# A fused attention and feed-forward kernel on one core: softmax 576 wide, values in 128-token chunks, another planner

## Chip, cores, metric

The kernel runs on one core of one Trainium2 chip. The metric is device time in microseconds (us), lower is better. Times are medians of several runs. In the profiles PE is TensorE (matmul), PEld its weight loads, DVE is VectorE, ACT is ScalarE, POOL is GpSimd and SP is the engine that issues most DMAs.

## The reference, cut to what matters

```python
# q, k, v: (8 batches, 8 heads, 576 tokens, 64); p: (8, 8, 32, 64); float32
def sm_attn(qq, kk, vv):
    s = scale * matmul(qq, kk.T)                  # scale = 1/8
    a = exp(s - max(s)); a = a / (sum(a) + 1e-9)
    return matmul(a, vv)
p_packed = sm_attn(p, k, v)                       # first softmax, over 576 tokens
x = sm_attn(q, p_packed, p_packed)                # second softmax, over 32 packed tokens
h = maximum(x @ w_in, 0)                          # x as (4608, 512), w_in (512, 2048)
out = (h * h) @ w_out                             # (2048, 512)
```

The kernel never forms `x`. Per batch it computes M = p_packed @ w_in once ("M chunks"), and the second softmax's weights times M give the hidden layer ("feed-forward groups" F1, 16 per batch). The squared result times w_out gives the output ("output matmuls" F2, 576 in all).

## The kernel before

A small planner inside the kernel takes steps with costs, dependencies and buffer slots, and decides in which order each engine gets its instructions. On the chip the order is then fixed.

```python
# sums of the first softmax, and what follows them (VectorE, in this order)
def extract(self):                       # packed values, PSUM -> SBUF, needed by M
    ...                                  # 4 copies of 64x64
def recip(self):
    nc.vector.reciprocal(self.rD, ps[:, 256:258])            # 128x2, from PSUM
    nc.vector.tensor_scalar_mul(self.rD8, self.rD, 0.125)    # 128x2, SBUF -> SBUF
def pq_block(self):                      # "block copies": operand of the second softmax
    ...                                  # 8 copies of 32x64, PSUM -> SBUF
# second softmax, per half (288 of 576 queries), PSUM tiles of one bank (pool "a")
S2:  ps_a <- pq, qT      exp(scale=rD8) on ScalarE -> e2
N:   ps_a <- ones_bd, e2  Ln, then Exp(scale=-1) on ScalarE; VectorE multiplies e2 by it
# feed-forward, PSUM tiles of two banks (pool "h", two tiles)
F1:  ps_h <- M, a2        relu on ScalarE (0.65 us) -> r;  gT = r*r on VectorE
F2:  ps_o <- gT, w_out    16 matmuls per 128 tokens
# casts of k, q, v to bf16 on GpSimd; v in 96-token chunks (6 groups)
```

The softmax here doesn't subtract the row's maximum and nothing guards it: scores larger than these inputs give would overflow.

## Time and profile before

The median was 286.82 us of 3 runs (285.31 to 287.47). The profiled execution itself took 288.86 us, so its absolute sums are a little high.

| | before |
|---|---|
| span of the profiled run | 287.1 us |
| TensorE busy | 248.8 us (87%) |
| VectorE / ScalarE / GpSimd busy | 183.8 / 173.6 / 78.3 us |
| TensorE matmuls | 1920 |

First the page of the kernel before: busy time by engine, and the TensorE and clock rows of the picture in 40 slices (tenths of each 7.2 us slice).

```profile
PE 248.8 (87%) x1920; PEld 141.1 (49%) x1920; DVE 183.8 (64%) x360; ACT 173.6 (60%) x333; POOL 78.3 (27%) x120
PE   0527958689969979997999799999999999999993
PEclk9999986979979999999999999999999999999999
```

The next table cuts the same run into stretches. Columns: start and end, length, busy time (and instructions) of TensorE, its weight loads, VectorE, ScalarE and GpSimd, then the granted clock, the DMA share and GB/s.

```profile
0.00:20.00 20.00, 4.55 (x60) 4.45 (x60) 12.45 (x33) 8.35 (x13) 7.13 (x23) 1.00 0.96 306
20.00:40.00 20.00, 15.52 (x136) 8.67 (x137) 15.44 (x25) 15.51 (x31) 8.72 (x7) 1.00 1.05 346
40.00:60.00 20.00, 14.54 (x86) 6.93 (x86) 17.72 (x31) 11.31 (x24) 11.00 (x11) 0.77 1.07 319
60.00:100.00 40.00, 37.27 (x309) 22.49 (x307) 32.79 (x53) 24.59 (x48) 24.99 (x47) 0.94 0.88 255
100.00:280.00 180.00, 174.53 (x1322) 97.72 (x1321) 105.38 (x221) 113.28 (x218) 26.42 (x35) 1.00 0.33 94
```

Length minus TensorE busy is the hole: 15.5, 4.5, 5.5, 2.7 and 5.5 us. From 60 us on TensorE is nearly full, so every hole there lengthens the run, and so does every matmul.

Who makes the holes after 40 us? These are TensorE's waits in that stretch (waiting line, what released it: total us, times, longest).

```profile
PE ps_a L365 <- DVE pq_bd_101 L339: 4.4, 3, 2.4
PE ps_o L422 <- POOL w_out_b L175: 3.5, 3, 2.5
PE ps_a L365 <- DVE pq_bd_102 L339: 3.5, 2, 1.8
PE ps_o L422 <- DVE gT L414: 2.3, 2, 1.3
```

The two lines with `pq_bd` are the second softmax (L365) waiting for VectorE's block copies: 7.9 us together. One such wait, in order of time, shows what delays the copies (start, duration, engine, line, instruction):

```profile
74.75 2.87 POOL L175 CAST v_b<-v_f 96x1536 bf16<-96x1536 f32 x2
74.97 0.17 DVE L329 RECIPROCAL rD<-ps_pp 128x2 f32<-128x2 f32 x1
75.17 3.57 DVE L330 TENSOR_SCALAR rD_1058<-rD 128x2 f32<-128x2 f32 x1
77.58 2.23 POOL L175 CAST q_b<-kq_f 128x1152 bf16<-128x1152 f32 x2
78.65 1.36 DVE L279 STREAM_TRANSPOSE kT<-k_b 128x1152 bf16<-128x1152 bf16 x1
79.95 1.83 DVE L339 CAST pq_bd_101<-ps_pp 32x64 bf16<-32x64 f32 x8
81.58 0.69 PE L365 MATMUL ps_a<-qT,pq_bd_101 128*128 128x288 bf16 x2 [2.42 <-DVE pq_bd_101 L339]
```

The multiply of 128x2 numbers is recorded at 3.57 us, the reciprocal of the same size just before it at 0.17. The multiply ends at 78.74; GpSimd's first q cast began at 77.58 and a q cast takes 1.14 us, so it ended at 78.72. The multiply sat through the rest of three GpSimd casts. This repeats in five of the eight batches (3.57, 3.17, 2.95, 3.13 and 1.91 us). In the first batch the multiply takes 0.96 us beside one cast, and in the other two 0.17, with no cast or one that was just ending. The cause of the meeting is in the program: the end of the value matmuls frees the v buffer for GpSimd's casts and gives VectorE its sums at the same moment.

The hole that ends at 81.58 us has a second cost. Here are two stretches, just before and just after its end (columns as in the table above), and two groups of matmuls 288 wide, the first within the second stretch and the other after it:

```profile
78.20:81.60 3.40, 0.98 (x6) 0.26 (x4) 3.29 (x10) 0.07 (x1) 3.40 (x4) 1.00 1.00 257
81.60:85.00 3.40, 3.40 (x15) 2.09 (x16) 2.24 (x6) 1.69 (x4) 0.40 (x1) 0.51 1.03 262
82.54 2.13 PE L399 MATMUL ps_h<-a_662,M 128*128 128x288 bf16 x8
85.56 0.65 PE L399 MATMUL ps_h<-a_662,M 128*128 128x288 bf16 x4
```

After the hole the granted clock was 0.51 for 3.4 us. TensorE was busy all that time, but its matmuls started 240 ns apart; the later four started 122 to 123 ns apart. So a busy TensorE can lose time too: a stretch whose clock is under 1.00 holds less work than its busy time says.

### The profile page before, as it was taken

Reading aid. Unit: us, or ns where it says so; the run is one execution under the profiler, and the core shown is the slowest. Engines: PE = TensorE matmul, PEld = TensorE weight load, DVE = VectorE, ACT = ScalarE, POOL = GpSimd, SP = SyncE. Lnnn points to the kernel's source line nnn. Section 1 sums busy time; section 2 is a strip of 40 time slices with the busy share of each in tenths; the row PEclk is TensorE's granted clock in tenths of the full one; section 3 lists DMA queues with packets and bytes.
Section 4 is the critical chain, followed back from the end, with each engine's and each line's share of the span. In section 5 each row is a group of like instructions: output and inputs, shape, how many; then the busy total and the mean of one; then the engine's idle time right before and its main releaser. Section 6 shows DMA issues by size and latency. Waiting matters only on the chain.

```text
span 287.1 us, 5281 instructions
## 1 busy us (share of the span) xinstructions
PE 248.8 (87%) x1920; PEld 141.1 (49%) x1920; DVE 183.8 (64%) x360; ACT 173.6 (60%) x333; POOL 78.3 (27%) x120
## 2 busy tenths in 40 slices
PE   0527958689969979997999799999999999999993
PEld 0512624346535634573547354755566555654441
DVE  4595978896967877769685968597744742520000
ACT  3628936767538557983877398659729864731110
POOL 5041674568940830029002900150000000000000
PEclk9999986979979999999999999999999999999999
DMA  7999999999997479012961392110211112112322
GB/s 235 294 410 370 285 388 379 226 327 232 322 257 307 103 194 335 13 38 69 294 233 48 93 275 64 49 37 22 55 39 37 39 37 73 30 47 73 75 73 73
DMA packets 23865, 47.00 MB, mean 164 GB/s; under 512 B 5920, under 2 KB 12064, under 8 KB 23840
## 3 DMA queue, kind: packets, MB, share of 16 engines
q1 hardware_dynamic: 23312, 46.55, 54.4%
q8 instruction: 15, 0.25, 0.4%
q10 hardware_dynamic: 528, 0.13, 0.2%
q14 instruction: 10, 0.08, 0.1%
HBM read 37.22 MB, written 9.44 MB: 163 GB/s over the span
## 4 chain that ended last, share of the span: by engine, by line
PE 57%; DVE 23%; DMA 8%; ACT 6%; issue 2%; SPq 2%; POOL 0%; ACTq 0%
PE ps_o L422 31%; PE ps_h L399 15%; DVE kT L279 6%; PE ps_a L365 4%; DMA w_f<-in_moe_w_out_dram 4%; DVE gT L414 3%; PE ps_a L349 3%; DMA v_f<-in_v_dram 2%; DVE pq_bd_101 L339 2%; DVE qT L273 2%; PE ps_a L289 2%; DMA out_dram<-o_sb 2%; ACT r L407 2%; PE ps_a L376 1%; DVE ppT L323 1%
## 5 line engine op out<-in xcount | busy, mean ns | idle before, releaser
L422 PE MATMUL ps_o<-w_out_b,gT 128*128 128x512 bf16 x576 | 146.0, 382 | 5.8 <-POOL w_out_b L175 3.5
L407 ACT ACTIVATE r<-ps_h 128x576 bf16<-128x576 f32 x125 | 78.5, 651 | 18.1 <-PE ps_h L399 12.9
L422 PEld LDWEIGHTS <-gT 128*128 128x128 bf16 x576 | 55.9, 98 | 61.2 <-issue 8.9
L414 DVE TENSOR_TENSOR gT<-r 128x576 bf16<-128x576 bf16 x128 | 64.0, 522 | 33.7 <-ACT r L407 32.0
L399 PEld LDWEIGHTS <-M 128*128 128x128 bf16 x512 | 49.8, 101 | 25.4 <-issue 4.0
L173 ACT COPY o_sb<-ps_o 128x512 f32<-128x512 f32 x25 | 14.7, 587 | 40.9 <-DMA out_dram<-o_sb 23.0
L357 ACT ACTIVATE M<-ps_a,rD 128x512 bf16<-128x512 f32 x46 | 30.1, 686 | 10.0 <-PE ps_a L349 9.4
L175 POOL CAST v_b<-v_f 96x1536 bf16<-96x1536 f32 x14 | 20.7, 1496 | 25.6 <-PE ps_pp L313 20.4
L273 DVE STREAM_TRANSPOSE qT<-q_b 128x1152 bf16<-128x1152 bf16 x16 | 21.9, 1370 | 1.6 <-POOL q_b L175 1.4
L279 DVE STREAM_TRANSPOSE kT<-k_b 128x1152 bf16<-128x1152 bf16 x16 | 21.9, 1368 | 0.8 <-issue 0.6
L289 PEld LDWEIGHTS <-kT 128*96 128x96 bf16 x192 | 14.6, 132 | 11.8 <-DVE kT L279 7.3
L175 POOL CAST k_b<-kq_f 128x1152 bf16<-128x1152 f32 x14 | 15.8, 1143 | 10.9 <-DMA kq_f<-in_k_dram 10.0
L349 PE MATMUL ps_a<-w_in_b,ppT 64*32 64x512 bf16 x256 | 16.3, 413 | 2.4 <-ACT M L357 1.7
L359 DVE TENSOR_SCALAR M<-ps_a,rD 128x512 bf16<-128x512 f32 x18 | 13.5, 748 | 6.0 <-PE ps_a L349 5.9
L365 PE MATMUL ps_a<-qT,pq_bd_101 128*128 128x288 bf16 x32 | 7.8, 347 | 10.9 <-DVE pq_bd_101 L339 10.0
L289 PE MATMUL ps_a<-pT_bd_99,kT 128*96 128x128 bf16 x96 | 8.0, 241 | 10.1 <-DVE pT_bd_99 L175 7.9
L175 POOL COPY pT_bd_100<-pT 32x64 bf16<-32x64 bf16 x32 | 7.3, 254 | 33.9 <-PE ps_a L289 30.8
L175 POOL CAST q_b<-kq_f 128x1152 bf16<-128x1152 f32 x14 | 15.9, 1151 | 1.2 <-DMA kq_f<-in_q_dram 1.2
L380 ACT ACTIVATE ls<-ps_a 128x288 f32<-128x288 f32 x32 | 13.2, 412 | 2.1 <-PE ps_a L376 2.0
L384 ACT ACTIVATE rs<-ls 128x288 f32<-128x288 f32 x32 | 14.1, 443 | 0.2
L175 POOL COPY pT_bd_99<-pT 32x64 bf16<-32x64 bf16 x24 | 6.4, 292 | 25.8 <-PE ps_a L289 24.5
L349 PEld LDWEIGHTS <-ppT 64*32 64x32 bf16 x256 | 4.1, 90 | 17.2 <-issue 15.7
(182 smaller groups left out, 263.3 us busy)
## 6 DMA issues: line engine op xcount, KB each, us to landing
kq_f<-in_k_dram SPq DMA_DIRECT2D x16, 576.0 KB, 7.5
v_f<-in_v_dram SPq DMA_DIRECT2D x48, 192.0 KB, 5.9
kq_f<-in_q_dram SPq DMA_DIRECT2D x16, 576.0 KB, 7.1
out_dram<-o_sb SPq DMA_DIRECT2D x144, 64.0 KB, 1.7
w_f<-in_moe_w_in_dram SPq DMA_DIRECT2D x8, 512.0 KB, 9.0
w_f<-in_moe_w_out_dram SPq DMA_DIRECT2D x8, 512.0 KB, 10.4
w_f<-in_p_dram SPq DMA_DIRECT2D x1, 384.0 KB, 8.6
w_f<-in_p_dram ACTq DMA_DIRECT2D x1, 128.0 KB, 4.0
```

What stands on the lines that cost most here:

```text
L173: nc.scalar.copy(dst, src)
L175: eng.tensor_copy(dst, src)
L273: nc.vector.transpose(self.qT[:, qd].rearrange("p dh (j a) -> p j dh a", a=32), self.t.qb[qd][:].rearrange("p (j dh dl) -> p j dh dl", dh= ...
L279: nc.vector.transpose(self.kT[:, qd].rearrange("p dh (g jp a) -> p jp g dh a", jp=JP, a=32), self.t.kb[qd][:].rearrange("p (jp g dh dl) -> ...
L289: nc.tensor.matmul(ps[:JP * 32, gi * P:(gi + 1) * P], lhsT=lhsT, rhs=pT_bd[self.b % 2][:, (qd * 2 + dh) * P:(qd * 2 + dh + 1) * P], start= ...
L349: nc.tensor.matmul(pss[qd][o:o + 32, :], lhsT=self.ppT[64 * e:64 * e + 64, qd, pr, :], rhs=w_in_b[64 * e:64 * e + 64, qd * 2 + pr, c * WCH ...
L357: nc.scalar.activation(dst, self.psm[c][e], ACT.Copy, scale=self.rD[:, e:e + 1])
L365: nc.tensor.matmul(ps[:, :HALF], lhsT=self.pq[:, (qd * 2 + dh) * P:(qd * 2 + dh + 1) * P], rhs=self.qT[:, qd, dh, n0:n0 + HALF], start=(dh ...
L399: nc.tensor.matmul(ps[:, c, :HALF], lhsT=a.M[:, qd, fb * FB:(fb + 1) * FB], rhs=a.a2[:, qd, c * HALF:(c + 1) * HALF], start=(qd == 0), sto ...
L407: nc.scalar.activation(dst, src, ACT.Relu)
L414: eng.tensor_tensor(out=gT[:, fb, o:o + S], in0=r, in1=r, op=ALU.mult)
L422: nc.tensor.matmul(po[t], lhsT=gT[:, fb, n0:n0 + P], rhs=w_out_b[:, fb, :], start=(fb == 0), stop=(fb == NFB - 1))
```

## The change

Its intent: fewer and fuller matmuls, fewer and wider ScalarE instructions in the second softmax, and a planner that packs better. The diff, cut to its core (the planner's 250 new lines are left out but for the choice rule):

```diff
-JP = 3; G = 6                      # values and scores in 6 chunks of 96 tokens
+GM = 4; REM = 64                   # 4 chunks of 128 and a rest of 64, padded with zeros
-            nc.vector.memset(ones_c, 1.0)
+            nc.vector.memset(ones_c, 8.0)              # rD is now 1/(8*sum)
-    nc.gpsimd.memset(ones_bd[...], 1.0)
+    nc.gpsimd.memset(ones_bd[...], 0.125)
-                nc.vector.tensor_scalar_mul(self.rD8, self.rD, 0.125)
 # second softmax: 576 wide, in the two-bank tiles of the feed-forward
-                ps = ps_att.tile([P, 512], F32, name="ps_a", tag="a")      # per half
+                ps = ps_h.tile([P, 2, 512], F32, name="ps_s", tag="h")     # whole
+        WIDE = tuple(range(B))      # batches done wide: all
 # after the sums: block copies first, half of them on ScalarE or VectorE; then reciprocal, then extract
-  stage([("DVE", 1.05, extract + recip)]), stage([("DVE", 1.85, pq_block)])
+  stage([("DVE", 0.92, pq_block(0))], [("DVE", 0.92, pq_block(1, V)), ("ACT", 1.2, pq_block(1, A))],
+        [("DVE", 0.2, recip)], [("DVE", 0.75, extract)])
 # w_in: 8 loads of 128 rows x 1024 columns -> 8 loads of 256 rows x 512 columns
 # key transpose: one instruction -> two (1024 and 128 columns)
 # values: 6 DMAs of 1536-byte pieces per batch -> 4 of 1024-byte and 2 of 256-byte pieces
 # planner: of the steps that may start within 0.03 us, the most urgent -> lowest start + 0.003*priority;
 #          a step may be booked into an earlier gap of its engine
-            c = min((c for c in cand if c[0] <= t0 + self.near), key=lambda c: (c[1], c[0], c[2]))
+            s = t if e == "-" else gap(e, us, t)[0]
+        ROUNDS = 0; SEEDS = ()      # no search; the count of dummy matmuls is also zero
 # casts of k, v, q: one stream -> three; batch 0 may cast on GpSimd too; output group 0 its own stream
```

## The prediction

> **What bounds it now.** The page of before: span 287.1 us, TensorE busy 248.8 (87%), VectorE 183.8, ScalarE 173.6, GpSimd 78.3. From about 100 us on TensorE is saturated (stretches table: 176.9 busy of 182 between 100 and 282 us), and it ends with 88 output matmuls in a row (chain of waits: 19.0 us), then 4.7 us of output copy and DMA. So the time is TensorE work plus holes. Holes, same table: 15.4 us before 20 us (loads; DMA share over 1), 4.5 from 20 to 40, about 13.6 from 40 to 282. The granted clock was 0.66 in 40–50, 0.89 in 50–60 and 0.83 in 80–90. The Trainium skill, "TensorE: Matmul & The Clock Gate", says that idle windows throttle the clock; the dips here follow holes of 1 to 2.5 us. At full-clock spacings (0.216 us per output matmul, 0.122 per 288-wide one, 0.056 per score matmul) the work is about 243 us, so slow clock costs some 6 us.
>
> **Costs of the change.**
> - 128-token chunks: 32 fewer score matmuls (0.056 each), 48 fewer in values and sums (0.043 to 0.048): 4 us of TensorE, fully on the critical path.
> - Softmax 576 wide: 96 activations of 288 (0.50, 0.41, 0.44 us) become 48 of 576; the relu of that shape takes 0.65. ScalarE saves about 12 us, and 2–3 on the first exponentials; at 60% busy only its latency counts.
> - The 0.125 scaling moves into constants, so the 128x2 VectorE multiply goes. It is recorded at 2–3.6 us in five batches while GpSimd casts beside it (the reciprocal before it takes 0.17). The skill, "SBUF — State Buffer", says that VectorE and GpSimd take a shared port pair as an exclusive lock; these durations agree. It stands ahead of the second softmax, which waits 2.4 us at 81.6 and again near 102, 136 and 164 us. Block copies now come first, half of them on ScalarE.
> - w_in arrives in column quarters: the first M chunk needs two loads instead of four.
> - The planner fills gaps; its fill count of dummy matmuls is zero. 13 feed-forward groups of batch 0 now stand before the first output matmul, against 11.
> - Costs: values arrive as 1024 and 256 byte pieces instead of 1536; the second softmax shares the two feed-forward PSUM tiles; the key transpose becomes two instructions.
>
> **Sum.** About 40 us still pass before w_out lands: the loads ahead of it are the same bytes. Work done by then rises by 1 us or less. Afterwards before lost 15 us to holes and slow clock over 242 us. I expect roughly half back, mostly between 40 and 60 us and at batch starts. 286.8 − 4 (fewer matmuls) − 7 (holes, clock) − 1 = 275.5 us (rounded). Range 268 to 282. Chances: faster by over 2% 0.83, within 2% 0.14, slower 0.03.
>
> **What would show it.** TensorE matmuls 1840; busy near 241; ScalarE near 158; VectorE 160 to 168 with no 128x2 multiply; TensorE busy over 8.5 of 10 us in 40–50 and 50–60, clock over 0.85; waits of the second softmax on the block copies under 1 us in later batches; a tail of about 135 output matmuls, ended some 11 us sooner.
>
> **What would make it wrong.** The order on each engine is fixed: if planned durations are off, the packed order stalls TensorE where before had slack, above all at the shared PSUM tiles (then: waits of the second softmax or the feed-forward on ScalarE, and no gain over the 4 us). If 40–60 us is bound by w_out landing, those holes stay: 279 to 282. If the clock stays full and holes nearly vanish, about 268.

## The result, and the profile after

The kernel after took 274.35 us, median of 4 runs (273.34 to 275.70), against 287.14 us for the kernel before, median of 4 (285.31 to 289.54). The ratio is 0.955, 95% interval 0.947 to 0.964. Ratios are the mean time of one kernel's fast runs over that of the other's fast runs of the same rounds, so they are not quite the ratio of the medians quoted. A second measurement of the unchanged kernel, beside later experiments, gave 275.91 us and 0.968 (0.962 to 0.973). So the change is worth 9 to 13 us.

The page of the kernel after, same rows:

```profile
PE 243.0 (90%) x1840; PEld 135.4 (50%) x1840; DVE 172.7 (64%) x325; ACT 168.6 (62%) x302; POOL 82.7 (30%) x127
PE   0436967999989999999999999999999999999992
PEclk9999999999999999999999999999999999999997
```

Its stretches:

```profile
0.00:20.00 20.00, 5.43 (x54) 4.04 (x55) 10.97 (x32) 7.58 (x14) 8.77 (x29) 1.00 0.93 264
20.00:40.00 20.00, 14.87 (x112) 7.47 (x112) 14.99 (x25) 11.61 (x19) 6.09 (x6) 1.00 1.08 328
40.00:60.00 20.00, 17.55 (x141) 8.99 (x138) 19.87 (x32) 13.69 (x25) 12.80 (x11) 1.00 1.08 334
60.00:100.00 40.00, 38.86 (x326) 21.98 (x324) 34.86 (x59) 27.07 (x53) 29.55 (x50) 1.00 0.96 271
100.00:264.00 164.00, 163.78 (x1213) 91.91 (x1206) 91.99 (x181) 108.10 (x192) 25.47 (x34) 1.00 0.39 104
```

Holes now: 14.6, 5.1, 2.5, 1.1 and 0.2 us. Up to 40 us nothing is gained (19.7 us against 19.9). Between 40 and 60 us 3.0 us are gained, from 60 to 100 us 1.6, and after 100 us 5.3: there TensorE is now simply full. These are holes alone. The clock rose as well, from 0.77 (40 to 60 us) and 0.94 (60 to 100 us) to 1.00; in the second profile of after it was 0.91 from 20 to 60 us and 1.00 from then to 100 us.

TensorE's waits after 40 us in the kernel after:

```profile
PE ps_h L612 <- DVE r L622: 1.2, 1, 1.2
PE ps_a L473 <- POOL pT_bd L342: 1.0, 2, 0.8
PE ps_a L542 <- DVE ppT L342: 0.7, 2, 0.5
PE ps_o L636 <- DVE w_out_b L342: 0.3, 1, 0.3
```

The waits of the second softmax on the block copies are gone from the list. What remains is small.

One group went the other way, the squares on VectorE. First the line of before, then that of after (count, then busy and mean ns, then idle before):

```profile
L414 DVE TENSOR_TENSOR gT<-r 128x576 bf16<-128x576 bf16 x128 | 64.0, 522 | 33.7 <-ACT r L407 32.0
```

```profile
L627 DVE TENSOR_TENSOR gT<-r 128x576 bf16<-128x576 bf16 x128 | 71.1, 580 | 28.6 <-ACT r L620 27.7
```

### The profile page after: what moved, and what is told of

Same layout as the page of the kernel before. It is cut to its first block, busy times and chain, and to the rows that moved or that the text cites. A ratio compares the mean times of both kernels' runs of the same rounds, so it can differ in the third digit from the quotient of the medians.

```text
span 271.4 us, 5108 instructions
## 1 busy us (share of the span) xinstructions
PE 243.0 (90%) x1840; PEld 135.4 (50%) x1840; DVE 172.7 (64%) x325; ACT 168.6 (62%) x302; POOL 82.7 (30%) x127
## 4 chain that ended last, share of the span: by engine, by line
PE 60%; DVE 18%; DMA 11%; SPq 4%; ACT 2%; issue 2%; POOL 1%; DVEq 0%; POOLq 0%; ACTq 0%
PE ps_o L636 31%; PE ps_h L612 17%; DVE gT L627 6%; DMA v_f<-in_v_dram 4%; DMA kq_f<-in_k_dram 4%; DMA out_dram<-o_sb 3%; DVE qT L455 3%; PE ps_a L542 3%; PE ps_s L572 3%; SPq L645 3%; PE ps_a L473 2%; DVE a L600 2%; PE ps_pp L507 2%; DVE M L552 2%; ACT o_sb L340 1%
## 5 line engine op out<-in xcount | busy, mean ns | idle before, releaser
L612 PE MATMUL ps_h<-a,M 128*128 128x288 bf16 x512 | 82.1, 292 | 2.2 <-DVE r L622 1.2
L342 POOL CAST q_b<-kq_f 128x1152 bf16<-128x1152 f32 (+1 forms) x16 | 19.7, 1244 | 25.5 <-DMA kq_f<-in_q_dram 25.2
L342 POOL CAST v_b<-v_f 128x1280 bf16<-128x1280 f32 (+1 forms) x15 | 18.8, 1279 | 27.1 <-PE ps_pp L511 10.1
L461 DVE STREAM_TRANSPOSE kT<-k_b 128x1024 bf16<-128x1024 bf16 x16 | 19.8, 1235 | 5.7 <-PE ps_a L487 4.8
L342 POOL CAST k_b<-kq_f 128x1152 bf16<-128x1152 f32 (+1 forms) x15 | 17.7, 1180 | 13.5 <-DMA kq_f<-in_k_dram 9.4
L473 PE MATMUL ps_a<-pT_bd,kT 128*128 128x128 bf16 x128 | 10.0, 230 | 11.0 <-DVE pT_bd L342 8.3
L342 POOL COPY pT_bd<-pT 32x64 bf16<-32x64 bf16 x56 | 13.5, 267 | 10.9 <-PE ps_a L487 8.8
L579 ACT ACTIVATE e<-ps_s,rD 128x576 bf16<-128x576 f32 x16 | 11.4, 739 | 5.8 <-PE ps_s L572 5.7
L572 PE MATMUL ps_s<-qT,pq_bd 128*128 128x288 bf16 x64 | 11.0, 306 | 3.1 <-ACT pq_bd L340 1.8
L600 DVE TENSOR_TENSOR a<-e,rs 128x576 bf16<-128x576 bf16 x16 | 13.6, 848 | 0.0
```

Of the source, the lines that this page charges most:

```text
L342: eng.tensor_copy(dst, src)
L461: nc.vector.transpose(self.kT[:, qd, :, :GM * P].rearrange("p dh (g jp a) -> p jp g dh a", jp=4, a=32), self.t.kb[qd][:, :JM * D].rearrang ...
L473: nc.tensor.matmul(ps[:, g * P:(g + 1) * P], lhsT=self.kT[:, qd, dh, g * P:(g + 1) * P], rhs=pT_bd[self.b % 2][:, (qd * 2 + dh) * P:(qd * ...
L612: nc.tensor.matmul(ps[:, c, :HALF], lhsT=a.M[:, qd, fb * FB:(fb + 1) * FB], rhs=a.a2[:, qd, c * HALF:(c + 1) * HALF], start=(qd == 0), sto ...
```

## The experiments

The change bundles at least five things. Undoing or doing one at a time shows what each is worth. Runs of one group share the chip and the runs of before; the unchanged kernel after ran again in the second group. A plan made anew is another order on every engine, so where an edit touches the planner's input the experiment compares orders as well. Whether the order stayed is said each time; it was checked by comparing the built programs. After itself ran with the result and in the second group only, so the other groups are compared with it by their ratios to before, 0.955 and 0.968.

**A build that needed no run: gap filling.** The planner's `gap` was replaced by "start after the last booked step of the engine":

```diff
-                    s = t if e == "-" else gap(e, us, t)[0]
+                    s = t if e == "-" else max(t, busy.setdefault(e, ([-1.0], [0.0]))[1][-1])
```

The built program is the same, instruction for instruction, on all five engines. Steps are taken nearly in order of their start times, and then there is no earlier gap to fill. So the gap filling of the change does nothing here, and it was not run.

**The multiply gone, from the kernel before (order kept).** This is the change's constant folding alone: `ones_c` 8.0, `ones_bd` 0.125, exponential scaled by rD, and

```diff
-                nc.vector.tensor_scalar_mul(self.rD8, self.rD, 0.125)
```

> The kernel before with only the 128x2 VectorE multiply gone (0.125 moved into the constants as in the change); every engine's order is otherwise the same. Theory A (the multiply waits for GpSimd on the shared port and holds the second softmax, whose TensorE waits for the block copies after 40 us sum to some 8 us): those waits fall below 2 us, VectorE busy falls by about 16 us, time falls by 5 to 8 us (ratio 0.972 to 0.983). Theory B (the delay only moves to the next instruction that needs the port, or the queued output matmuls hide it): under 2 us (ratio above 0.993).

Measured: 276.89 us against 285.19 (ratio 0.974, 0.969 to 0.978): 7.5 us saved, worked out as (1 − 0.9737) × 285.19. After 40 us no wait of the second softmax on the block copies is left. VectorE busy fell only from 183.8 to 179.2, not by 16: the squares rose to 73.7 us (600 ns each). So both theories hold a part. Waiting did move to other VectorE instructions beside GpSimd's, as theory B says: in both traces a square that met no GpSimd instruction took at most 0.46 us, and the 25 that met one in before became 31 here, the longest 2.5 us. But there it holds TensorE for only 1.5 us in all after 40 us, and the time falls as theory A says.

**The same instruction slot, but reading PSUM (kernel before, order kept).** To tell "a 128x2 multiply between SBUF operands" from "any VectorE instruction at that place":

```diff
-ones_c = consts.tile([JP * 32, 1], ...)             # 1.0
+ones_c = consts.tile([JP * 32, 2], ...)             # columns 1.0 and 8.0
-nc.vector.tensor_scalar_mul(self.rD8, self.rD, 0.125)
+nc.vector.reciprocal(self.rD8, <the column of 8*sum in PSUM>)
```

> The kernel before with the 128x2 multiply replaced by a second 128x2 reciprocal that reads PSUM (the sums matmul gets a second column of 8.0), at the same place, with the same dependency. If the multiply cost time because its operands lie in SBUF and VectorE then waits for GpSimd (shared port), the replacement is recorded at 0.17 us in all eight batches and the time is as e5_before_no_mult, ratio 0.967 to 0.98. If any extra VectorE instruction there stalls, it is recorded at 2 to 3 us again and the ratio is above 0.99.

Measured: 276.89 us against 286.42 (ratio 0.970, 0.965 to 0.975), 8.6 us saved. The second reciprocal never stalled. The lines give the least, median and longest duration in ns:

```profile
L330 DVE RECIPROCAL rD<-ps_pp x8: 170/171/172, 16.2 to 200.8; 128x2 f32<-128x2 f32 x8
L331 DVE RECIPROCAL rD<-ps_pp x8: 149/150/151, 16.3 to 200.9; 128x2 f32<-128x2 f32 x8
```

Same engine, shape and place in the order: 0.15 us instead of up to 3.57. Two things differ at once: it is a reciprocal and not a multiply, and it reads the sums in PSUM and not the result of the instruction before it in SBUF. The profile of after tells the two apart. There VectorE does 25 multiplies that read PSUM (the M chunks), 10 of them beside GpSimd casts, and none is held up:

```profile
L552 DVE TENSOR_SCALAR M<-ps_a,rD x25: 734/750/752, 22.4 to 203.5; 128x512 bf16<-128x512 f32 x25
```

The stretches of this run show where the time came back:

```profile
40.00:60.00 20.00, 14.55 (x104) 7.40 (x104) 18.48 (x33) 12.49 (x27) 11.82 (x11) 0.91 1.07 322
60.00:100.00 40.00, 38.88 (x323) 23.70 (x321) 36.14 (x66) 27.18 (x57) 28.08 (x49) 1.00 0.90 264
100.00:267.00 167.00, 167.00 (x1289) 94.69 (x1287) 97.27 (x206) 108.66 (x208) 24.17 (x32) 1.00 0.35 98
```

The hole of 40 to 60 us is as before (5.5 us). Those of 60 to 100 and after 100 us fell from 2.7 and 5.5 to 1.1 and 0: 7.1 us, the size of the 7.9 us of waits that are gone. So this one instruction closes as much hole after 60 us as the whole change does (6.9 us). Holes are not all of it: with the same 1920 matmuls TensorE busy fell from 248.8 to 244.1 us. The clock column accounts for most of that. As an estimate, its missing share times the busy time is 0.23 × 14.54 + 0.06 × 37.27 = 5.6 us in before and 0.09 × 14.55 = 1.3 us here. The two parts sum to more than the 8.6 us because the profiled run of before was slow (288.86 us).

**The multiply back into the kernel after (order kept).** The constants and the multiply as before, behind the reciprocal.

> The kernel after with the 128x2 multiply put back behind the reciprocal, all orders otherwise the same. Theory A: it is recorded at 2 to 3 us in some batches, the second softmax waits for it, and the time rises by 3 to 8 us (274 to 278-282). Theory B: VectorE busy rises but the time stays within 1 us.

Measured: 277.57 us, ratio 0.973 (0.967 to 0.979), against 0.955 and 0.968 for after: by these ratios 1.5 to 5 us more. Neither theory's numbers hold. The multiply is recorded at 0.17 to 0.79 us, never at 2 to 3:

```profile
L526 DVE TENSOR_SCALAR rD<-rD x8: 168/400/794, 17.9 to 200.6; 128x2 f32<-128x2 f32 x8
```

In the new order the block copies stand before the reciprocal, and the multiply meets GpSimd's casts for less long: in the six batches where it meets one, it ended with that cast. After 40 us TensorE shows no wait of the second softmax for it. This profile has a clock of 0.88 and 0.86 in 20 to 40 and 40 to 60 us; whether the multiply or the scatter cost the 1.5 to 5 us is not shown. The short durations suggest that moving the multiply in the kernel before would have cured most of the stall too, but no run tried that.

**80 matmuls put back (kernel after, order kept).** Redundant score, value and sum matmuls of the sizes that the change removed:

```diff
+    for x in range(2): for dh in range(2): matmul(ps[:, x*P:(x+1)*P], kT, pT_bd)   # overwritten later
+    for x in range(2): matmul(ps[:, 320+64*x:384+64*x], v, e1)                     # unused columns, per half
+    matmul(ps[:, 300:301], e1, ones_c)
```

> The kernel after with 80 redundant matmuls (per batch 4 score matmuls of 128x128, 4 value matmuls 64 wide, 2 sums of width 1), written to PSUM columns that are overwritten or unused; orders otherwise the same. If TensorE work is fully on the critical path (prediction), the time rises by 4 us (32 x 0.056 + 32 x 0.043 + 16 x 0.048 = 3.9) give or take 1. If they fall into holes, by under 2 us.

Measured: 277.38 us, ratio 0.972 (0.966 to 0.979), by the ratios 1.3 to 4.8 us above the two measurements of after. The profile fell in a slow run and lacks 31 matmul records. Its TensorE busy is 246.0 us, against 241.8 in the second profile of after, which lacks 30: 4.2 us more work. The time agrees with "on the critical path", but the scatter does not rule out "under 2 us".

**The second softmax 288 wide (planned anew).** The planner's own switch, `WIDE = ()`, nothing else.

> The kernel after with the second softmax done 288 wide in one-bank tiles (the planner's own switch), all else as after; the order is planned anew. Theory C (the wide softmax shortens the chain of the softmax and is part of the gain): ScalarE busy rises by 10 to 12 us, time rises by 2 to 5 us. Theory D (ScalarE has slack, so only the removed matmuls, the multiply and the order matter): ScalarE busy rises as much, the time stays within 1 us.

Measured: 287.76 us, ratio 1.007 (0.999 to 1.014). The whole gain is gone, far more than theory C's 2 to 5 us. ScalarE rose from 168.6 to 180.1 us, as both theories said, but it is not the bound. TensorE's hole between 80 and 100 us is 4.8 us (0 in after), and these are its waits from 60 to 110 us:

```profile
PE ps_o L636 <- DVE gT L627: 5.9, 6, 2.6
PE ps_a L572 <- ACT e L579: 1.1, 2, 0.6
```

Output matmuls wait for squares. In that stretch squares and GpSimd's casts overlap, and three squares are recorded at 3.97 us together instead of 1.37 (three times the median of 0.458). No queue of ready output matmuls was left to hide this: at 88.63, 90.06 and 91.37 us one output matmul each ran right behind the square that it had waited for. Is that the width, or an accident of this order?

**The same, with another order.** The planner's cost of a square was set to 0.58 us (0.48 before), near what the traces show.

> The 288-wide softmax (as e1_narrow, 287.8 us) planned again with one changed number: the planner's cost of a square 0.58 us instead of 0.48, near the 0.58 to 0.60 us mean that the traces show. If e1_narrow was slow because 288-wide work as such costs 13 us, it stays above 284. If e1_narrow was slow because its planned order put output matmuls straight behind squares that GpSimd's casts then delayed (an accident of that order), it falls to 276 to 281.

Measured: 282.93 us, ratio 0.990 (0.986 to 0.995), between the two expectations. Some 5 us of e1_narrow were the order; the rest stayed.

**288 wide, but in the two-bank tiles (planned anew).**

```diff
-            pool, m = ("h", 2) if wide else ("a", 1)
+            pool, m = ("h", 2) if wide else ("h", 1)
```

> The kernel after with the second softmax 288 wide, but in the two-bank feed-forward tiles (one bank of each used), planned anew. Compare e1_narrow (287.8 us) and e6_narrow_sq58 (282.9), 288 wide in the one-bank tiles. If the gain of the wide softmax is one of place (it leaves the one-bank tiles to M and the scores), the time is 274 to 278. If it is one of width (half as many steps and hand-overs per batch), it stays at 281 to 288.

Measured: 280.95 us, ratio 0.983 (0.976 to 0.989), at the edge of the two expectations and nearer to "width". All three 288-wide versions lie 5 to 12 us above after (275.91), and all three have a hole of 3.5 to 4.8 us between 80 and 100 us with the output matmuls waiting for squares (4.0 us in e6_narrow_sq58, 3.0 in this one, between 60 and 110 us). So in the orders tried the width is worth 5 to 7 us in the new kernel, and 12 where an unlucky order came on top; no run parts it wholly from the order. How much the place in PSUM adds cannot be told from orders that differ.

**The kernel after with another order.** The square at 0.58 us, nothing else.

> The kernel after planned again with a square at 0.58 us. It measures how much the time depends on the order alone: if the order hardly matters when the softmax is wide, 273 to 276; if orders are a lottery, it may lie anywhere from 270 to 285. A better-matched cost should not be worse: guess 273.

Measured: 275.91 us, ratio 0.966 (0.961 to 0.972), the same as after in its group (275.91, 0.968). With the wide softmax this other order costs nothing. The unchanged kernel, for that comparison:

> The kernel after, unchanged, as the baseline of this group. Expected 273 to 276 us, ratio to before 0.955 to 0.97.

Measured: 275.91 us (275.16 to 279.15), ratio 0.968. Two of its runs had mean granted clocks of 0.983 and 0.994 and took 275.92 and 275.90 us.

**The old planner's choice and streams, with all new instructions.**

```diff
-  key = greedy(pc, t) + 0.003 * prio;  best = lowest key
+  best = most urgent of those that start within 0.03 us of the earliest
-  three cast streams, (A, V, Q) for batch 0; output group 0 its own stream
+  one cast stream, (A, V) for batch 0; one output stream
```

> The kernel after with the choice rule of the old planner (of the steps that could start within 0.03 us of the earliest, the most urgent stream), one stream of casts on ScalarE and VectorE for batch 0, and one stream of output groups: all instructions as after, the order nearly that of the old planner. If the planner and streams are part of the gain: 277 to 284. If not: 273 to 276.

Measured: 280.51 us, ratio 0.981 (0.976 to 0.987), 4.6 us above after by the medians. Its holes are 15.4, 6.0, 4.9, 3.1 us up to 100 us, against 14.6, 4.5, 2.7, 2.1 in the second profile of after. TensorE's waits from 20 to 110 us begin with

```profile
PE ps_s L574 <- DVE qT L457: 5.0, 2, 4.3
PE ps_a L475 <- POOL pT_bd L344: 2.6, 1, 2.6
```

that is, query transposes and GpSimd copies that come late. So the rule and the streams are worth some 4 us in the first 100 us, through what comes first, not through filled gaps.

**w_in in halves again (kernel after).** The loads and casts of before; M chunk c waits for four loads.

> The kernel after with w_in loaded and cast as before: eight loads of one 128-row block by 1024 columns, so that the first M chunk needs four loads. The prediction gave the quarters 1 us or less. Expected: M starts 2 to 3 us later in batch 0, the time 274 to 278, within 1.5 us of after.

Measured: 273.75 us, ratio 0.960 (0.954 to 0.966). The first M matmul starts at 21.7 us in both, not 2 to 3 us later as was expected. The quarters bring nothing that can be seen.

**A version meant to beat both.** No relu on VectorE in batch 0, w_out casts on ScalarE or GpSimd, ScalarE allowed for w_in, square cost 0.58.

```diff
-        NDV = 1
+        NDV = 0
-  w_in_cast((Q, V)) + w_out_cast((Q, V))
+  w_in_cast((Q, V, A)) + w_out_cast((A, Q))
```

> An attempt at a version that beats both: after, with no relu on VectorE in batch 0, the w_out casts on ScalarE or GpSimd instead of GpSimd or VectorE, ScalarE allowed for w_in casts, square cost 0.58. VectorE is 95% busy in 40 to 60 us and ScalarE 62%. If VectorE bounds that stretch, TensorE holes there shrink by 2 to 4 us and the time is 271 to 273. If the loads bound it, 275 to 277.

Measured: 276.92 us (272.93 to 280.91; three of the six runs were slow), ratio of the fast runs 0.963 (0.955 to 0.970). VectorE fell from 19.9 to 15.4 us busy in 40 to 60 us, and TensorE's hole there is 3.6 us, not smaller. VectorE's load does not bound that stretch, and no version tried is clearly better than after.

## Why the prediction was right

The time (275.5 predicted, 274.35 and 275.91 measured) and the direction were right. Point by point:

- *What bounds it*: right. The time follows TensorE work plus holes. The forecast tail of about 135 output matmuls is there (135, ended at 266.6 us), but before had one of 136 too (ended at 282.4): it ends sooner and did not grow.
- *4 us of removed matmuls*: in the right direction, 1.3 to 4.8 us when put back, not resolved better. TensorE busy is 243.0 us, not 241, and only 1.1 us under that of the run with the second reciprocal, which has all 1920 matmuls; why it did not fall further is open.
- *The multiply that waits for GpSimd*: right in mechanism and place in the kernel before. The Trainium skill, "SBUF — State Buffer", section "Who interferes with whom", says that a VectorE instruction in a two-port mode and a GpSimd instruction exclude each other for whole instructions, and names the scalar multiply among those that can enter such a mode. This agrees: 1.9 to 3.6 us with SBUF operands in five batches, 0.15 us with a PSUM operand in all eight, and no multiply out of PSUM over 0.752 us. Its size was not stated; it is 7.5 to 8.6 us alone, which is more than the prediction gave to all holes and clock together (7 us). That 7 was "roughly half" of 15 and not worked out from this multiply, so it is partly luck that it came so close. Of the change's 9 to 13 us it leaves 0.4 to 5.5 to all the rest, where the prediction had 5.
- *"mostly between 40 and 60 us and at batch starts"*: both places gave. After 60 us 6.9 of the 9.9 us of closed holes came back, between 40 and 60 us 3.0. Of clock, by the estimate above, 3.3 us came back between 40 and 60 us and 2.2 after (first profile of after). The multiply closes none of the holes of 40 to 60 us; other versions of after that keep the wide softmax and the new choice rule have 2.6 to 3.7 us there.
- *"The planner fills gaps"*: wrong. The append-only build is identical. The planner's choice rule and streams are still worth some 4 us, which the prediction had not put in.
- *"Only its latency counts"* of the wide softmax: right that ScalarE time does not count, but no figure was given for the latency; undone, the width costs 5 to 12 us.
- *w_in quarters*: 1 us or less predicted, nothing seen.
- *Slow clock costs some 6 us*: supported as an estimate (5.6 us by the clock column, as worked out above), and part of it came back with the multiply. The Trainium skill, "TensorE: Matmul & The Clock Gate", section "What's actually happening", says that the clock is halved after an idle window. This agrees: 0.51 and 240 ns between matmuls after the hole at 81.58 us, against 122 to 123. No run changes the clock alone. In each of the three groups of 11 runs of before, a mean clock lower by 0.01 goes with 1.2 to 2.6 us more (a fitted line), but single pairs scatter: two runs of after at mean clocks of 0.983 and 0.994 took the same time.
- *ScalarE near 158 us, VectorE 160 to 168 us*: missed, 168.6 and 172.7. The wide exponential takes 739 ns, not the 650 of the relu, because it takes its scale from a 128x1 operand. The Trainium skill, "ScalarE: Activation LUTs", section "What ACT_TABLE_LOAD costs", says that each such operand adds about 93 ns; here it is 739 − 651 = 88, or 1.4 us for all 16. The larger part is that half of the block copies now run on ScalarE (6.5 us), which the sum had left out. VectorE's miss is mostly the squares, 7.1 us longer than in the kernel before; the two kernels that only lost the multiply show the same (73.4 and 73.7 us against 64.0).
- *TensorE over 8.5 of 10 us in 40–50 and 50–60, clock over 0.85*: 8.13 and 9.41, so missed in the first and met in the second; the clock was 1.00.

The terms do not add up. The multiply alone gives 7.5 to 8.6 us of the 9 to 13; the fewer matmuls, the width and the planner's choice each cost 1 to 12 us when undone alone in the new kernel. A likely reason is the queue of ready output matmuls in the first 100 us, which each undone part may drain. That this queue couples them was argued from the waits, not isolated by a run. Nor did a run undo the new place of the block copies or their share on ScalarE alone. Why the kernel before, also 288 wide, does not suffer as e1_narrow does stays open: their orders differ.

## What to carry to other kernels

Look for tiny VectorE instructions with large recorded durations: a two-column multiply between SBUF operands waited for three GpSimd casts and cost 3% of the time; here folding the constant elsewhere cured it, and so did reading PSUM instead. Read the clock column beside busy time: a hole can slow the work that follows it. When a static scheduler changes, build with its new feature off first and compare the programs: here the named feature changed no instruction. And a part's value measured by undoing it in the new kernel is not its share of the gain; do it alone in the old kernel too.

## What the Trainium skill lacked or had wrong

- "SBUF — State Buffer", summary table, says that the second to issue blocks until the first finishes. Here it blocked for longer: the multiply issued during one GpSimd cast ended only with the third cast in a row (75.17 to 78.74 us, the casts from 74.75 on at 1.46, 1.46 and 1.14 us). The page does not say that back-to-back GpSimd instructions can keep the waiting VectorE instruction out. They do not always: in the kernel after with the multiply put back, it ended with the first cast in three batches in which the next cast followed at once.
- No page says how much of a wait that is taken away returns at other VectorE instructions: with the multiply gone from the kernel before, its squares rose from 522 to 600 ns on average.
- "TensorE: Matmul & The Clock Gate", section "What's actually happening", gives the slow state as coming after at least one idle window of about 3.4 us. Here a window that was only partly idle was enough: TensorE was busy 0.98 of the 3.40 us before the clock fell to 0.51 at 81.6 us, and its longest wait in them was 2.42 us.
